# A decode step of attention and a gated MLP on one core: the last 192 rows of w_down loaded as 104 and 88 whole rows

## The chip, the cores and the metric

The kernel runs on one core of one Trainium2 chip. The metric is the device time of one execution in microseconds, as the median of several runs. All profile lines come from one profiled execution of the same program; times in them count from the start of its span.

## The reference, cut to what matters

```python
x = A_x                                                   # 1 x 640, bf16
h = x + A(layernorm(x), k_cache, v_cache, wq, wo)         # 32 heads, 4096 cached keys, head size 128
g, u = layernorm(h) @ w_gate, layernorm(h) @ w_up         # 640 -> 1728
h2 = h + (gelu(g) * u) @ w_down                           # 1728 -> 640
```

One token is computed. The two caches are 32 MB each, wq and wo 5 MB each, and the three MLP weights 2.2 MB each, so that 84 MB are read once and there is little arithmetic on each byte.

## The kernel before, in words

The order of the work is written out by hand: `Prog` (`P`) keeps one list of operations for each engine, `P.dma` adds a load, `V`, `A`, `T` and `GP` add work of VectorE, ScalarE, TensorE and GpSimd, and `emit` writes the lists out with one semaphore for each load. An operation waits for the events it is given. Within a list nothing overtakes.

All big loads are issued by SyncE, at line 59, in this order: wq into `arena`; sixteen K and V blocks of 4 MB into three `slots` in turn, the last V block in two halves; wo in three parts; and the MLP weights into the slots that have come free (`free[0]`, `free[1]`). A K block is multiplied by q on VectorE (L295), summed by TensorE against an identity (L28, L305), reduced (L313) and put through exp (L317); a V block is multiplied on TensorE (L336) and picked apart on VectorE (L353 to L363). Then come the projection by wo (L404), the sum with x, a layernorm (L258 to L264, L498) and the MLP.

The MLP's loads are issued in this order: two w_down loads for the rows from 1536 on (`d_wd[0]`, `d_wd[1]`), w_gate (`d_wg`), w_up in two parts (`d_wu`), and the first 1536 rows of w_down in four parts (`d_wd[2]` to `d_wd[5]`), the last of which is 128 rows of 1280 bytes. `wd_sb` holds w_down as 14 columns of 128 partitions by 640 numbers; columns 0 to 11 are the first 1536 rows.

`glu` (L509) makes g and u as rows, `turn` (L515 to L522) copies a row to SBUF and turns it by small matmuls into columns, 14 columns of 128 partitions. Lines 537 to 546 make gelu(g) times u, in `hm`, of 128 by 14. `down` (L553) multiplies column m of `hm` with column m of `wd_sb` and adds up in PSUM, as four pieces of 160 numbers. Two copies on VectorE (L566) and two on ScalarE (L568) bring the result to SBUF, and one store writes it.

In the kernel before, column 12 holds rows 1536 to 1663. The last 64 rows, of 1280 bytes each, are loaded as 128 half rows of 640 bytes, so that partition 2f has the first and partition 2f+1 the second half of row f. For that the 64 values of column 13 of `hm` are spread by one matmul with `sel2` over 128 partitions (`hp`, L557) and masked by `par` into the two columns of `hm2` (`h2`, L559), one for even partitions and one for odd ones. `sel2`, `par_t` and `par` are made at the start (L235, L238, L247). `z0` and `z1` (L496, L497) clear the part of column 13 that no matmul of `turn` writes.

Of the kernel before, what the change touches and what calls it, by code (L numbers as in the profile page):

```python
# [5 lines left out]
FP32 = mybir.dt.float32  # L6
BF16 = mybir.dt.bfloat16
ALU = mybir.AluOpType
ACTF = mybir.ActivationFunctionType
AX = mybir.AxisListType  # L10
# [8 lines left out]
GELU_C0 = math.sqrt(2.0 / math.pi)  # L19
GELU_C1 = 0.044715  # L20
NG = 8
NSLOT = 3


# [85 lines left out]
def bass_sequential_preLN__gqa_block_cached__glu_gated_geglu__decode_kernel(nc, A_x, A_k_cache, A_v_cache, A_wq, A_wo, B_x, B_w_gate, B_w_up, B_w_down, out):  # L110
    sb = lambda name, shape, dt: nc.alloc_sbuf_tensor(name, shape, dt)
    SLOT = 10 * DF
    slots = [sb("slot%d" % i, [128, SLOT], BF16) for i in range(NSLOT)]
    arena = sb("arena", [128, 5 * 4096], BF16)
    prod = sb("prod", [128, 4, 32, DH], BF16)
    qb = sb("qb", [128, NG, DH], BF16)
    sc = sb("sc", [128, 4, 32], FP32)
# [22 lines left out]
    rows = [sb("rows%d" % i, [128, 512], BF16) for i in range(2)]  # L140
    sel4 = sb("sel4", [128, 4], BF16)
# [4 lines left out]
    e_t = sb("e_t", [128, 14], FP32)  # L146
    gu = sb("gu", [128, 14], FP32)
    hm = sb("hm", [128, 14], BF16)
    hm2 = sb("hm2", [128, 2], BF16)
    sel2 = sb("sel2", [64, 64, 2], BF16)  # L150
    par_t = sb("par_t", [128, 2, 64], BF16)
    par = sb("par", [128, 2], FP32)
    one_bf = sb("one_bf", [1, 1], BF16)
    ones_f = sb("ones_f", [128, 128], FP32)
    mean_f = sb("mean_f", [128, 128], FP32)
    ones_b = sb("ones_b", [128, 1024], BF16)
# [9 lines left out]
    ps_g, ps_u = bank[0], bank[1]  # L166
    ps_q = [bank[4], bank[7]]
    ps_a = bank[4]
    ps_d = bank[4][:, 256:416]
    ps_s = bank[5]  # L170
    ps_z = bank[6]
    ps_p = bank[7]

    wo_sb = arena[:, :].rearrange("p (t i n) -> p t i n", t=2, i=16)
    view = lambda n: slots[n % NSLOT][:, 0:128 * DH].rearrange("p (g d) -> p g d", d=DH)

    P = Prog(nc)
    V = lambda fn, *d: P.op("vector", fn, *d)
    A = lambda fn, *d: P.op("scalar", fn, *d)
    T = lambda fn, *d: P.op("tensor", fn, *d)  # L180
    GP = lambda fn, *d: P.op("gpsimd", fn, *d)
# [4 lines left out]
    d_wq = [P.dma("sync", arena[:, :], A_wq[:, :].rearrange("(p c) n -> p (c n)", c=5))]  # L186
    order = [(kind, G) for G in range(NG - 2) for kind in "KV"] + [(kind, G) for kind in "KV" for G in (NG - 2, NG - 1)]
    pos = {t: n for n, t in enumerate(order)}
# [8 lines left out]
    def issue(upto):  # L197
        while state["next"] < min(upto, len(order)):
            n = state["next"]
            kind, g = order[n]  # L200
            src = A_k_cache if kind == "K" else A_v_cache
            src = src[0, 4 * g:4 * g + 4, :, :].rearrange("h (p r) d -> (h p) (r d)", p=32)
            dst = slots[n % NSLOT][:, 0:128 * DH]
            parts = 2 if n == len(order) - 1 else 1
            w = 128 * DH // parts
            landed[n] = [P.dma("sync", dst[:, i * w:(i + 1) * w], src[:, i * w:(i + 1) * w], consumed[n - NSLOT] if n >= NSLOT else None)
                         for i in range(parts)]
            state["next"] = n + 1

    issue(NSLOT)  # L210

# [6 lines left out]
    c_onesb = GP(lambda e: e.memset(ones_b[:, :], 1.0))  # L218
    c_idb = GP(lambda e: e.affine_select(id_b[:, :], ones_b[:, 0:128], pattern=[[1, 128]], compare_op=ALU.is_equal,
                                         fill=0.0, base=0, channel_multiplier=-1), c_onesb)  # L220
    c_idf = GP(lambda e: e.affine_select(id_f[:, :], ones_f[:, :], pattern=[[1, 128]], compare_op=ALU.is_equal,
                                         fill=0.0, base=0, channel_multiplier=-1), c_ones)
    c_sel = GP(lambda e: e.affine_select(sel[:, :, :], ones_b[0:16, :].rearrange("p (a b) -> p a b", a=8),
                                         pattern=[[-1, 8], [1, 128]], compare_op=ALU.is_equal,
                                         fill=0.0, base=0, channel_multiplier=-8), c_onesb)
    c_hz = GP(lambda e: e.memset(hs[:, :], 0.0))
    c_hs = GP(lambda e: e.affine_select(hs_t[:, :, :], ones_f[:, :].rearrange("p (a b) -> p a b", a=4),
                                        pattern=[[-1, 4], [-4, 32]], compare_op=ALU.is_equal,
                                        fill=0.0, base=0, channel_multiplier=1), c_ones)
    c_s4 = GP(lambda e: e.affine_select(sel4[:, :], ones_b[:, 0:4], pattern=[[-32, 4]], compare_op=ALU.is_equal,  # L230
                                        fill=0.0, base=0, channel_multiplier=1), c_onesb)
    c_m8 = GP(lambda e: e.affine_select(m8_t[:, :, :, :], ones_f[:, :].rearrange("p (a b c) -> p a b c", a=8, b=4),
                                        pattern=[[-4, 8], [-32, 4], [-1, 4]], compare_op=ALU.is_equal,
                                        fill=0.0, base=0, channel_multiplier=1), c_ones)
    c_sel2 = GP(lambda e: e.affine_select(sel2[:, :, :], ones_b[0:64, 0:128].rearrange("p (a b) -> p a b", a=64),  # L235
                                          pattern=[[1, 64], [0, 2]], compare_op=ALU.is_equal,
                                          fill=0.0, base=0, channel_multiplier=-1), c_onesb)
    c_par = GP(lambda e: e.affine_select(par_t[:, :, :], ones_b[:, 0:128].rearrange("p (a b) -> p a b", a=2),  # L238
                                         pattern=[[-1, 2], [-2, 64]], compare_op=ALU.is_equal,
                                         fill=0.0, base=0, channel_multiplier=1), c_onesb)  # L240
    c_pbd = GP(lambda e: e.memset(p_bd[:, :, :, :], 0.0))

    c_hs = V(lambda e: e.reduce_sum(hs[:, 12:16], hs_t[:, :, :], axis=AX.X), c_hs, c_hz)
    c_o4 = V(lambda e: e.reduce_max(ones4[:, :], sel4[:, :], axis=AX.X), c_s4)
    c_m8 = V(lambda e: e.reduce_sum(m8[:, :], m8_t[:, :, :, :].rearrange("p a b c -> p a (b c)"), axis=AX.X), c_m8)

    V(lambda e: e.reduce_sum(par[:, :], par_t[:, :, :], axis=AX.X), c_par)  # L247


    def x_cols(e):  # L250
# [20 lines left out]

    wq_j = arena[:, :].rearrange("p (c g j d) -> p c j g d", c=5, g=NG, j=4)

# [74 lines left out]
    def p_sum(G):  # L348
        sums[G] = V(lambda e: e.reduce_sum(RT[:, 4 * G:4 * G + 4], p_bd[:, G % 2, :, :].rearrange("p g j -> p j g"), axis=AX.X),  # L349
                    exps[4 * G + 3])  # L350
# [6 lines left out]
    def pick_sum(G):  # L357
        if G >= NG - 2:
            a1 = V(lambda e: e.tensor_add(po_m[:, 0:4, :], po_m[:, 0:4, :], po_m[:, 4:8, :]), mks[G])
# [56 lines left out]
    def scores(G):  # L416
# [7 lines left out]
        if G > 0:  # L424
            p_sum(G - 1)
        issue(pos[("K", G)] + 1 + NSLOT)

    headed = 0
    for kind, G in order:
# [14 lines left out]
        if G == 5:  # L444
# [10 lines left out]
    free = [consumed[len(order) - NSLOT + i] for i in range(1, 3)]  # L455
    wg_sb = sl[0][:, 0:5 * DF].rearrange("p (c n) -> p c n", c=5)
    wu_sb = sl[0][:, 5 * DF:10 * DF].rearrange("p (c n) -> p c n", c=5)
    wd_sb = sl[1][:, 0:14 * D].rearrange("p (m n) -> p m n", m=14)
    wu_v = B_w_up[:, :].rearrange("(p c) n -> p c n", c=5)
    wd_v = B_w_down[0:1536, :].rearrange("(a p r) n -> p a r n", a=3, r=4)  # L460
    wd_d = wd_sb[:, 0:12, :].rearrange("p (a r) n -> p a r n", a=3)
    d_wd = [P.dma("sync", wd_sb[:, 12, :], B_w_down[1536:1664, :], free[1]),
            P.dma("sync", wd_sb[:, 13, 0:320], B_w_down[1664:1728, :].rearrange("f (s n) -> (f s) n", s=2))]
    d_wg = P.dma("sync", wg_sb, B_w_gate[:, :].rearrange("(p c) n -> p c n", c=5), free[0])
    d_wu = [P.dma("sync", wu_sb[:, 0:3, :], wu_v[:, 0:3, :]),
            P.dma("sync", wu_sb[:, 3:5, :], wu_v[:, 3:5, :])]
# [2 lines left out]

    p_sum(NG - 1)  # L470
    pick(NG - 1)
    pick_sum(NG - 1)
# [10 lines left out]
    lo = [V(lambda e, t=t: e.tensor_sub(A_lo[0:97, 320 * t:320 * t + 320], bank[t][0:97, 0:320], A_hi[0:97, 320 * t:320 * t + 320]),  # L483
            hi[t]) for t in range(2)]
# [8 lines left out]
    T(columns(A_hi, True), *hi, c_o4)  # L493
    pr = T(columns(A_lo, False), *lo)
    h = V(lambda e: e.tensor_add(hT[:, 0:5], xx[:, 0:5], ps_p[:, 0:5]), pr)
    z0 = V(lambda e: e.memset(ps_g[64:128, 13:14], 0.0), lo[0])  # L496
    z1 = V(lambda e: e.memset(ps_u[64:128, 13:14], 0.0), lo[1])  # L497
    hl = layernorm(hT, h, lambda e: e.tensor_scalar(  # L498
        hlnT[:, :], hT[:, 0:5], ln[:, 0:1], ln[:, 4:5], ALU.subtract, ALU.mult))
    hx = V(lambda e: e.tensor_tensor(out=hX[:, :, :], in0=id_f[:, :].unsqueeze(2).to_broadcast([128, 128, 5]),  # L500
# [13 lines left out]
    def turn(k, ps, ev, z):  # L514
        cp = (V, A)[k](lambda e: (e.copy if k else e.tensor_copy)(rows[k][0:97, :], po[0:97, 512 * k:512 * k + 512]), ev)  # L515

        def fn(e):
            for r in range(4):
                i = e.matmul(ps[:, r:12:4], rows[k][0:97, r::4], sel4[0:97, 0:3], start=(r == 0), stop=True, skip_group_check=True)
            for m in (12, 13):  # L520
                n = 128 if m < 13 else 64
                i = e.matmul(ps[0:n, m:m + 1], rows[k][0:97, 128 * (m - 12):128 * (m - 12) + n], sel4[0:97, 3:4],  # L522
                             start=False, stop=True, skip_group_check=True)
            return i
        return T(fn, cp, z, c_s4)
# [20 lines left out]
    g9 = V(lambda e: e.tensor_mul(hm[:, :], gu[:, :], ps_u[:, 0:14]), g6, up)  # L546

    def down(ms, qs=range(4)):
        def fn(e):
            for m in ms:  # L550
                for q in qs:
                    h, n = (hm[:, m:m + 1], 160 * q) if m < 13 else (hm2[:, q // 2:q // 2 + 1], 160 * (q % 2))
                    i = e.matmul(ps_d[32 * q:32 * q + 1, 0:160], h, wd_sb[:, m, n:n + 160],  # L553
                                 start=False, stop=(m == 11))
            return i
        return fn
    hp = T(lambda e: e.matmul(ps_z[:, 0:1], sel2[:, :, :].rearrange("p a b -> p (a b)"), hm[0:64, 13:14],  # L557
                              start=True, stop=True), g9, c_sel2)
    h2 = V(lambda e: e.tensor_mul(hm2[:, :], par[:, :], ps_z[:, 0:1].to_broadcast([128, 2])), hp)  # L559
    T(down([12]), d_wd[0])  # L560
    T(down(range(4)), d_wd[2])
    T(down([13]), h2, d_wd[1])
    T(down(range(4, 8)), d_wd[3])
    T(down(range(8, 11)), d_wd[4])
    dn = {q: T(down([11], [q]), d_wd[5]) for q in (0, 2, 1, 3)}
# [36 lines left out]
```

## Time and profile before

| | us |
|---|---|
| median of 3 runs | 203.08 (203.05 to 203.18) |
| the profiled execution, its own time | 202.97 |
| its span, first to last instruction | 201.7 |
| TensorE busy in the span | 115.3 |
| VectorE busy | 129.5 |
| ScalarE busy | 51.3 |
| share of 16 DMA engines' time taken by the loads of SyncE | 97.9% |
| data read | 84.23 MB, 418 GB/s over the span |

The span is what the profile's lines cover; the execution's own time has 1.27 us more around it. The DMA engines are busy nearly all of the span, and every other engine has gaps. The loads of SyncE are shown as SPq lines at the time of their issue; a wait for data is shown as a wait on DMA with the name of the tile and the tensor.

### The profile page before, as it was taken

Reading aid. Unit: us, or ns where it says so; the run is one execution under the profiler, and the core shown is the slowest. Engines: PE = TensorE matmul, PEld = TensorE weight load, DVE = VectorE, ACT = ScalarE, POOL = GpSimd, SP = SyncE. Lnnn points to the kernel's source line nnn. Section 1 sums busy time; section 2 is a strip of 40 time slices with the busy share of each in tenths; the row PEclk is TensorE's granted clock in tenths of the full one; section 3 lists DMA queues with packets and bytes.
Section 4 is the critical chain, followed back from the end, with each engine's and each line's share of the span. In section 5 each row is a group of like instructions: output and inputs, shape, how many; then the busy total and the mean of one; then the engine's idle time right before and its main releaser. Section 6 shows DMA issues by size and latency. Waiting matters only on the chain.

```text
span 201.7 us, 1568 instructions
## 1 busy us (share of the span) xinstructions
PE 115.3 (57%) x788; PEld 17.0 (8%) x384; DVE 129.5 (64%) x136; ACT 51.3 (25%) x139; POOL 5.6 (3%) x15
## 2 busy tenths in 40 slices
PE   0108059536737775197529655876396097754564
PEld 0101000000001000000000001001000000121222
DVE  1300188517994898379857966896879979683341
ACT  2100003610560055005502440252025214500111
POOL 7300000000000000000000000000000000000000
PEclk9999756996996699859997978798569859997575
DMA  9999999999999999999999999999999999999992
GB/s 333 439 398 455 442 422 416 416 442 468 432 422 416 416 422 455 443 442 417 416 416 445 442 448 422 422 416 429 442 442 448 387 429 423 427 409 439 415 408 99
DMA packets 4330, 84.32 MB, mean 418 GB/s; under 512 B 482, under 2 KB 868, under 8 KB 1508
## 3 DMA queue, kind: packets, MB, share of 16 engines
q1 hardware_dynamic: 4322, 84.23, 97.9%
q8 instruction: 4, 0.07, 0.1%
q14 instruction: 2, 0.02, 0.0%
q10 hardware_dynamic: 2, 0.00, 0.0%
HBM read 84.23 MB, written 0.00 MB: 418 GB/s over the span
## 4 chain that ended last, share of the span: by engine, by line
DMA 52%; DVE 21%; PE 19%; issue 3%; ACT 2%; SPq 2%
DMA slot<-in_A_k_cache_dram 43%; DVE prod L295 16%; PE bank L28 13%; DMA slot<-in_B_w_down_dram 9%; DVE sc L313 3%; PE bank L336 3%; PE bank L305 2%; ACT p_bd L317 2%; SPq L59 2%; DVE po_r L363 1%; DVE po_m L353 1%; PE bank L553 0%; DVE out_row L566 0%; DVE RT L349 0%; DVE aP L393 0%
## 5 line engine op out<-in xcount | busy, mean ns | idle before, releaser
L295 DVE TENSOR_TENSOR prod<-slot,qb 128x4096 bf16<-128x4096 bf16 x32 | 72.4, 2283 | 24.3 <-DMA slot<-in_A_k_cache_dram 24.3
L317 ACT ACTIVATE p_bd<-sc,zero_t 32x32 bf16<-32x32 f32 x128 | 46.4, 362 | 107.7 <-DVE sc L313 106.5
L28 PE MATMUL bank<-prod,id_b 128*128 128x512 bf16 x224 | 68.6, 458 | 0.0
L305 PE MATMUL bank<-prod,id_b 128*128 128x512 bf16 x32 | 15.3, 477 | 45.2 <-DVE prod L295 45.1
L313 DVE TENSOR_REDUCE sc<-bank 128x32 f32<-128x512 f32 x32 | 22.0, 687 | 14.7 <-PE bank L28 14.7
L336 PE MATMUL bank<-slot,p_bd 128*32 128x512 bf16 x128 | 14.8, 448 | 15.0 <-ACT p_bd L317 13.8
L28 PE MATMUL bank<-slot,p_bd 128*32 128x512 bf16 x128 | 14.9, 453 | 0.0
L305 PEld LDWEIGHTS bank<-prod,id_b 128*128 128x128 bf16 x32 | 3.5, 109 | 108.6 <-DVE prod L295 108.6
L363 DVE TENSOR_REDUCE po_r<-po_m 128x128 f32<-128x1024 f32 x6 | 11.2, 1867 | 0.0
L353 DVE TENSOR_TENSOR po_m<-bank,m 128x1024 f32<-128x1024 f32 x8 | 9.7, 1214 | 0.6 <-PE bank L28 0.6
L280 PE MATMUL bank<-arena,xlnB 128*32 128x512 bf16 x20 | 3.3, 628 | 7.2 <-DMA arena<-in_A_wq_dram 7.2
L285 DVE CAST qb<-bank 128x512 bf16<-128x512 f32 x1 | 0.7, 692 | 10.0 <-PE bank L28 10.0
L336 PEld LDWEIGHTS bank<-slot,p_bd 128*32 128x32 bf16 x128 | 3.8, 106 | 35.7 <-ACT p_bd L317 26.1
L509 PE MATMUL bank<-slot,hlnT 128*1 128x512 bf16 (+1 forms) x40 | 4.0, 486 | 2.7 <-DVE hX L500 2.2
L349 DVE TENSOR_REDUCE RT<-p_bd 128x4 f32<-128x512 bf16 x8 | 5.4, 675 | 0.0
L252 PE MATMUL bank<-one_bf,x_row 1*128 1x1 bf16 x5 | 0.4, 177 | 7.1 <-DMA x_row<-in_A_x_dram 7.1
L369 PE MATMUL bank<-po_r,hs 128*16 128x128 f32 x16 | 3.4, 301 | 1.5 <-DVE po_r L361 1.5
L286 ACT CAST qb<-bank 128x512 bf16<-128x512 f32 x1 | 0.6, 586 | 10.4 <-PE bank L28 10.4
L28 PE MATMUL bank<-arena,xlnB 128*32 128x512 bf16 x20 | 3.2, 613 | 0.0
L404 PE MATMUL bank<-arena,aP 128*1 128x320 bf16 x32 | 2.5, 314 | 1.1 <-DMA arena<-in_A_wo_dram 1.1
L263 ACT ACTIVATE ln<-ln,eps_t 128x1 f32<-128x1 f32 x2 | 0.6, 294 | 9.4 <-DVE ln L261 9.4
L482 ACT CAST A_hi<-bank 97x320 bf16<-97x320 f32 x1 | 0.4, 426 | 9.8 <-PE bank L28 9.8
(87 smaller groups left out, 42.9 us busy)
## 6 DMA issues: line engine op xcount, KB each, us to landing
slot<-in_A_k_cache_dram SPq DMA_DIRECT2D x8, 4096.0 KB, 21.0
slot<-in_A_v_cache_dram SPq DMA_DIRECT2D x7, 4096.0 KB, 17.7
arena<-in_A_wq_dram SPq DMA_DIRECT2D x1, 5120.0 KB, 15.5
slot<-in_A_v_cache_dram SPq DMA_DIRECT2D x2, 2048.0 KB, 14.9
arena<-in_A_wo_dram SPq DMA_DIRECT2D x1, 2560.0 KB, 22.9
slot<-in_B_w_gate_dram SPq DMA_DIRECT2D x1, 2160.0 KB, 11.0
arena<-in_A_wo_dram SPq DMA_DIRECT2D x1, 1920.0 KB, 27.0
slot<-in_B_w_up_dram SPq DMA_DIRECT2D x1, 1296.0 KB, 13.7
```

What stands on the lines that cost most here:

```text
L28: return e.add_instruction(mybir.InstMatmult(name=nc.get_next_instruction_name(), engine=e.engine, start_tensor_calc=start, stop_tensor_ca ...
L59: ev = self.op(eng, lambda e: e.dma_start(out, in_), *deps, dma=True)
L295: m = V(lambda e: e.tensor_tensor(out=prod[:, s % 4, :, :], in0=kt[:, 32 * u:32 * u + 32, :], in1=qb[:, G, :].unsqueeze(1).to_broadcast([1 ...
L305: i = e.matmul(*args, start=True, stop=False)
L313: reds[s] = V(lambda e: e.reduce_sum(sc[:, s % 4, :], ps_f[s % 2][:, :].rearrange("p (g d) -> p g d", d=16), axis=AX.X), folds[s], exps.ge ...
L317: x = A(lambda e, j=j: e.activation(p_bd[32 * j:32 * j + 32, G % 2, 32 * (s % 4):32 * (s % 4) + 32, j], sc[32 * j:32 * j + 32, s % 4, :], ...
L336: return e.matmul(*args, start=(c < 4), stop=(c >= 12))
L349: sums[G] = V(lambda e: e.reduce_sum(RT[:, 4 * G:4 * G + 4], p_bd[:, G % 2, :, :].rearrange("p g j -> p j g"), axis=AX.X), exps[4 * G + 3])
L353: mks[G] = V(lambda e: e.tensor_tensor(out=po_m[:, :, :], in0=po[:, :].rearrange("p (b d) -> p b d", b=8), in1=m8[:, :].unsqueeze(2).to_br ...
L363: evs[G] = V(lambda e: e.reduce_sum(po_r[:, G % 2, :], po_m[:, :, :].rearrange("p b d -> p d b"), axis=AX.X), mks[G], hds.get(G - 2))
L369: return e.matmul(ps_a[0:16, 128 * (G // 4):128 * (G // 4) + 128], hs[:, 12 - 4 * g:28 - 4 * g], po_r[:, G % 2, :], start=(g == 0), stop=( ...
L509: i = e.matmul(po[32 * a:32 * a + 1, 512 * k:512 * k + n], hlnT[:, c:c + 1], w[:, c, 512 * a:512 * a + n], start=(c == 0), stop=(c == 4))
```

## The change

The 192 rows from 1536 on are loaded as 104 whole rows onto partitions 0 to 103 of column 12 and 88 whole rows onto partitions 0 to 87 of column 13. `turn` makes column 12 with 104 and column 13 with 88 values, `z0` and `z1` clear the upper 64 partitions of both columns ahead of it, and `down` sums over 104 and 88 partitions for these two. `hp`, `h2`, `hm2`, `sel2`, `par_t` and `par` go away. On TensorE `down([12, 13])` now stands first and waits for both loads.

```diff
+TAIL = ((1536, 104), (1640, 88))
...
-    c_sel2 = GP(lambda e: e.affine_select(sel2[:, :, :], ones_b[0:64, 0:128].rearrange("p (a b) -> p a b", a=64),
...
-    c_par = GP(lambda e: e.affine_select(par_t[:, :, :], ones_b[:, 0:128].rearrange("p (a b) -> p a b", a=2),
...
-    V(lambda e: e.reduce_sum(par[:, :], par_t[:, :, :], axis=AX.X), c_par)
...
-    d_wd = [P.dma("sync", wd_sb[:, 12, :], B_w_down[1536:1664, :], free[1]),
-            P.dma("sync", wd_sb[:, 13, 0:320], B_w_down[1664:1728, :].rearrange("f (s n) -> (f s) n", s=2))]
+    d_wd = [P.dma("sync", wd_sb[0:n, 12 + i, :], B_w_down[lo:lo + n, :], free[1]) for i, (lo, n) in enumerate(TAIL)]
...
-    z0 = V(lambda e: e.memset(ps_g[64:128, 13:14], 0.0), lo[0])
-    z1 = V(lambda e: e.memset(ps_u[64:128, 13:14], 0.0), lo[1])
+    z0 = V(lambda e: e.memset(ps_g[64:128, 12:14], 0.0), lo[0])
+    z1 = V(lambda e: e.memset(ps_u[64:128, 12:14], 0.0), lo[1])
...
-            for m in (12, 13):
-                n = 128 if m < 13 else 64
-                i = e.matmul(ps[0:n, m:m + 1], rows[k][0:97, 128 * (m - 12):128 * (m - 12) + n], sel4[0:97, 3:4],
+            for m, (lo, n) in zip((12, 13), TAIL):
+                i = e.matmul(ps[0:n, m:m + 1], rows[k][0:97, lo - 1536:lo - 1536 + n], sel4[0:97, 3:4],
...
+                k = 128 if m < 12 else TAIL[m - 12][1]
                 for q in qs:
-                    h, n = (hm[:, m:m + 1], 160 * q) if m < 13 else (hm2[:, q // 2:q // 2 + 1], 160 * (q % 2))
-                    i = e.matmul(ps_d[32 * q:32 * q + 1, 0:160], h, wd_sb[:, m, n:n + 160],
+                    i = e.matmul(ps_d[32 * q:32 * q + 1, 0:160], hm[0:k, m:m + 1], wd_sb[0:k, m, 160 * q:160 * q + 160],
...
-    hp = T(lambda e: e.matmul(ps_z[:, 0:1], sel2[:, :, :].rearrange("p a b -> p (a b)"), hm[0:64, 13:14],
-                              start=True, stop=True), g9, c_sel2)
-    h2 = V(lambda e: e.tensor_mul(hm2[:, :], par[:, :], ps_z[:, 0:1].to_broadcast([128, 2])), hp)
-    T(down([12]), d_wd[0])
+    T(down([12, 13]), g9, *d_wd[0:2])
     T(down(range(4)), d_wd[2])
-    T(down([13]), h2, d_wd[1])
```

More of the change, by code (lines that the diff above doesn't have):

```diff
@@ L148, in bass_sequential_preLN__gqa_block_cached__glu_gated_geglu__decode_kernel @@
     hm = sb("hm", [128, 14], BF16)
[L149 to L152, printed above, removed]
     one_bf = sb("one_bf", [1, 1], BF16)
@@ L234, in bass_sequential_preLN__gqa_block_cached__glu_gated_geglu__decode_kernel @@
                                         fill=0.0, base=0, channel_multiplier=1), c_ones)
-    c_sel2 = GP(lambda e: e.affine_select(sel2[:, :, :], ones_b[0:64, 0:128].rearrange("p (a b) -> p a b", a=64),
-                                          pattern=[[1, 64], [0, 2]], compare_op=ALU.is_equal,
-                                          fill=0.0, base=0, channel_multiplier=-1), c_onesb)
-    c_par = GP(lambda e: e.affine_select(par_t[:, :, :], ones_b[:, 0:128].rearrange("p (a b) -> p a b", a=2),
-                                         pattern=[[-1, 2], [-2, 64]], compare_op=ALU.is_equal,
-                                         fill=0.0, base=0, channel_multiplier=1), c_onesb)
     c_pbd = GP(lambda e: e.memset(p_bd[:, :, :, :], 0.0))
```

## The prediction

> **What bounds the kernel now.** I read the page's slices and queues first.
>
> ```profile
> DMA  9999999999999999999999999999999999999992
> GB/s 333 439 398 455 442 422 416 416 442 468 432 422 416 416 422 455 443 442 417 416 416 445 442 448 422 422 416 429 442 442 448 387 429 423 427 409 439 415 408 99
> DMA packets 4330, 84.32 MB, mean 418 GB/s; under 512 B 482, under 2 KB 868, under 8 KB 1508
> q1 hardware_dynamic: 4322, 84.23, 97.9%
> q10 hardware_dynamic: 2, 0.00, 0.0%
> ```
>
> The DMA engines are at nine tenths or more in 39 of 40 slices: the load stream never pauses, so its last load sets the end and work on other engines is cover. Next, from the end of the chain of waits (start, us, step):
>
> ```profile
> 180.84 18.22 DMA slot<-in_B_w_down_dram
> ```
>
> It ends at 199.06. Then the end of the timeline (start, us, instruction, and in brackets the idle time before it):
>
> ```profile
> 179.90 1.85 SPq L59 DMA_DIRECT2D slot<-in_B_w_down_dram  x4
> 196.83 0.17 PE L557 MATMUL bank<-hm,sel 64*128 64x1 bf16 x1 [0.33 <-DVE hm L546]
> 196.94 0.71 PE L553 MATMUL bank<-slot,hm 128*1 128x160 bf16 x24
> 197.04 0.16 DVE L559 TENSOR_TENSOR hm<-par,bank 128x2 bf16<-128x2 f32 x1 [0.27 <-PE bank L557]
> 197.95 0.70 PE L553 MATMUL bank<-slot,hm 128*1 128x160 bf16 x16 [0.30 <-DMA slot<-in_B_w_down_dram]
> 199.10 0.70 PE L553 MATMUL bank<-slot,hm 128*1 128x160 bf16 x16 [0.45 <-DMA slot<-in_B_w_down_dram]
> 199.49 0.09 PEld L553 LDWEIGHTS bank<-slot,hm 128*1 128x1 bf16 x4 [0.16 <-DMA slot<-in_B_w_down_dram]
> ```
>
> TensorE waits three times at its end for w_down, 0.30, 0.45 and 0.16 us; only four matmuls, the copies and the store follow the last landing.
>
> A load is done when every engine with a share of it is done. The trace keeps the sixteen increments of each load's semaphore. Of the last load (128 rows of 1280 B), in us of the span:
>
> ```
> 197.74 197.82 197.89 197.93 198.00 198.08 198.10 198.18
> 198.23 198.44 198.90 199.03 199.25 199.28 199.30 199.44
> ```
>
> Sixteen engines run each at its own pace, the last 1.70 us behind the first. The packets say why: an engine moves 40960 B in 1514 ns with no gap (27.05 GB/s; sixteen make 433), and four instruction loads of 16 KB, at 53.9, 109.7, 174.8 and 193.5 us, each put one engine some 1.5 us behind. It never catches up. So the end is the end of one late engine, and what counts is what that engine has to do.
>
> **The change, part by part.**
>
> The loads: bytes stay at 245,760. Before, each engine has eight packets of 1280 B and eight of 640 B. Their packets last 55 and 32 ns and overlap by a few ns; between the increments of consecutive loads an engine spends 0.44 us on the eight of 1280 B and 0.20 us on the eight of 640 B, 0.64 in all. How 104 and 88 rows are shared out no row shows. The two near ones: a 128-row load has sixteen semaphore packets, and the one-row load of x two packets in all (q10), one of data, one semaphore. So a load goes over as many engines as its rows fill with equal shares; the most for 104 is 13, with eight rows each, and for 88 is 11, with eight. [...]
>
> Counting both from the same first engine, engines 0 to 10 have sixteen packets of 1280 B, 0.88 us in place of 0.64: +0.24. Engines 11 and 12 have eight: -0.20. Engines 13 to 15 have none: -0.64. The last engine's place among them is not in the trace. [...] So each late one has 10 chances in 15 to be among 1 to 10. If the last is (two in three), +0.24. If it is spared, the next three, 199.25 to 199.30, are all spared in only one case in a hundred, so the end is 199.30 + 0.24 = 199.54, +0.10. The ends of this term are what six engines from 198.90 on allow when five of them sit in 11 to 15: 198.90 + 0.24 for the sixth, -0.30 at best; and +0.24. I take +0.24.
>
> Where the rows land: in every load before, each engine has its own eight partitions, always the same for a 128-row load. Shares of 13 and 11 are cut elsewhere, on 104 and 88 partitions, so a late engine writes 16 rows into partitions that other engines, most of them over 1.2 us ahead, are at that moment filling with w_gate at their full rate. Whether 27.05 GB/s is the limit of the engine or of the place written to, the trace cannot tell. If the engine's, nothing is added. If the place's, each of the two gets half, and the late engine's sixteen packets take 0.88 us more. The slowed neighbours have the time to spare. No row lies between; the nearest is the rate of all sixteen engines, equal to under 1% over 40960 B packets although each reads its own rows, which looks like a fixed limit on the path to SBUF. I lean to the upper end: three quarters, +0.66, ends 0 and 0.88. [...]
>
> Fewer engines than 13 and 11 would make this dearer: eight for both, as 13 and 11 rows each, is 24 packets or 1.32 us, +0.68 before any sharing; one engine, as for x, 192 packets of 55 ns, +9.9. The spread's floor is zero: 192 rows evenly are 12 packets, 0.66 for 0.64.
>
> SyncE: two issues at 177.62 take 0.81 us; the odd shape may cost what x's issue cost on ScalarE, 0.49 for 0.33, +0.16 each. The first engine reaches these loads at 181.46, and the w_gate issue behind them ends at 178.90, so 2.5 us cover it. The six loads behind shift with it, all issued by 181.7 and the last started at 196.8. Nothing on the path; without cover +0.32.
>
> TensorE and VectorE at the end: `hp` (0.17 us), its weight load (0.09) and `h2` (0.16) go. `down` ran on beside them from 196.94 and then waited 0.30 us for w_down, so they hid behind that load: 0; without it -0.3. `down([12, 13])` waits for both tail loads, which landed at 184.19 and 184.37, twelve us before `hm`: 0, and if it were late all of `down` would queue behind it. The turning matmuls (L522, 163 to 213 ns) change from 128 and 64 columns to 104 and 88, the memsets from 64x1 to 64x2 (0.06 us each), below 0.05 us either way, and the waits for w_down absorb it.
>
> The start: two selects on GpSimd (0.71 and 0.30 us, from 4.84) and a sum on VectorE (0.29, at 5.84) go. x lands at 7.08 and wq is waited for until 15.66, so 0; no more than 1.0 if that cover were gone.
>
> Sum: 0.24 + 0.66 = +0.90 on the last landing, with TensorE, the copies and the store behind it unchanged: 202.97 + 0.90 = 203.87 for a profiled execution. The median of the runs stands 0.11 above it: 203.98, say 204.0.
>
> **Rivals.** A measurement here tells 0.2%, 0.41 us, from no change.
>
> Uneven shares alone (0.28): the place costs nothing, the last engine pays 0.10 to 0.24: 203.2 to 203.3, within 0.2%. For it: each load of the trace keeps the same rate whatever its packet size. Against: no load of before has two engines at the same partitions.
>
> The late engines are spared (0.08): the change takes 0.64 us off three engines and 0.20 off two, and if the six late ones sit there, or a slightly shorter program moves an instruction load off the last one, the end comes sooner. Best by the shares alone -0.30, 202.8, from five of the six late engines in the top five places on. With the instruction load of 174.8 us on an engine with time to spare, five are late, 198.90 to 199.30: all in the top five places, they end by 199.03 - 0.20 = 198.83, -0.61, 202.5, past the bound. I price all of it as faster.
>
> Fewer engines (0.06): the shares are not 13 and 11 but at most 8, so the change does not keep the loads spread: +0.68 with free places, up to 205.3 with all 24 packets shared (+0.68 + 1.32 = +2.00, on 203.08 is 205.08), and +9.9 for one engine, 213.0.
>
> The forecast keeps 0.58: +0.5 to +1.12.
>
> **How the numbers follow.** 204.0 is the likeliest case. Slower is the forecast and the fewer engines, 0.64; same 0.28; faster 0.08. The forecast's own range is 203.6 to 204.2; the range 203.1 to 205.0 takes in the uneven shares above their middle and eight engines, and leaves out the gain, the lowest of the uneven shares and the one-engine end, together under 0.2.
>
> **What would show it.** Packets under 512 B: 482 less 5 for 104 and 3 for 88 rows is 474; under 2 KB, 796; in all 4258. Sixteen equal shares would leave 482. The increments of the first tail load would be thirteen, of the second eleven. Right: packets of 1280 B in the tail well over 55 ns on some engines, the chain's last DMA step ending near 199.96, TensorE still waiting for it. Uneven shares alone: packets stay at 55 ns and the last landing is 199.5 to 199.7. Wrong altogether: the last landing before 199.3, the wait of TensorE for w_down gone, or a pause in the DMA slices.

## The result, and the profile after

| | before | after |
|---|---|---|
| median of the runs, us | 203.11 (203.05 to 203.57, 6 runs) | 204.33 (204.16 to 204.47, 6 runs) |
| the profiled execution, us | 202.97 | 204.32 |
| its span, us | 201.7 | 203.1 |
| last increment of the last load, us of the span | 199.45 | 200.80 |

The changed kernel is slower: 1.0057 times the time of before (95% interval 1.0044 to 1.0070), +1.22 us in the medians and +1.35 in the two profiled executions. The load stream still ends the kernel. From the page of after, slices and packets:

```profile
DMA  9999999999999999999999999999999899999991
GB/s 363 403 421 458 413 413 433 445 458 420 410 413 452 458 426 413 421 439 434 452 413 423 420 439 452 433 413 433 426 439 458 381 426 448 406 387 376 406 410 76
DMA packets 4258, 84.32 MB, mean 415 GB/s; under 512 B 474, under 2 KB 796, under 8 KB 1436
q1 hardware_dynamic: 4250, 84.23, 97.8%
```

The bytes are the same, and the packets are 474, 796 and 4258, as 13 and 11 semaphore packets for the two loads ask. The 36th and 37th slice moved 387 and 376 GB/s, for 409 and 439 before. The same stretch of both kernels in the view by windows; the columns are the window, its length, busy time and count of each engine, TensorE's granted clock, the DMA engines' busy share and GB/s. The view counts a packet whole where it starts, so a share can pass 1. Before:

```profile
core 0: us, PE busy (x) PEld busy (x) DVE busy (x) ACT busy (x) POOL busy (x), PEclk, DMA share, GB/s
182.00:187.00 5.00, 2.60 (x43) 1.17 (x28) 1.73 (x7) 0.43 (x1) 0.00 (x0) 0.66 1.08 449
```

After:

```profile
182.00:187.00 5.00, 2.81 (x37) 0.77 (x22) 1.38 (x3) 0.42 (x1) 0.00 (x0) 0.56 1.07 358
```

The DMA engines are as busy, 1.07 for 1.08, and move a fifth less, 358 GB/s for 449. (With only the part of each packet that lies in the window it is 331 for 421, the same loss.) Those 91 GB/s over 5 us are 455 KB, or 1.1 us at the 418 GB/s of the whole span before: by this estimate most of the loss lies here. The end of the chain of waits of after, then from the timelines one line of before and the end of after:

```profile
180.78 19.62 DMA slot<-in_B_w_down_dram
```

```profile
183.77 0.43 PE L404 MATMUL bank<-arena,aP 128*1 128x320 bf16 x4 [0.53 <-DMA arena<-in_A_wo_dram]
```

```profile
184.79 0.43 PE L393 MATMUL bank<-arena,aP 128*1 128x320 bf16 x4 [0.41 <-DMA arena<-in_A_wo_dram]
...
198.65 1.50 PE L540 MATMUL bank<-slot,hm 104*1 104x160 bf16 x40 [0.33 <-DVE hm L533]
200.44 0.71 PE L540 MATMUL bank<-slot,hm 128*1 128x160 bf16 x16 [0.28 <-DMA slot<-in_B_w_down_dram]
200.85 0.09 PEld L540 LDWEIGHTS bank<-slot,hm 128*1 128x1 bf16 x4 [0.18 <-DMA slot<-in_B_w_down_dram]
```

The chain's DMA step ends at 200.40, 1.34 us later than before. The line of before and the first one of after are the projection's last part: it waits for the wo load that stands ahead of the changed ones in the queue and starts at 184.79, where before it started at 183.77. So a load of which nothing was changed already lands 1.02 us late.

The packets of the tail in the two traces (ns; the tail is the packets of the two loads for the left-over rows; w_gate is the load behind them, the third part of wo the one ahead):

```
                        before                after
tail, 1280 B            128, mean 55,  max 58   192, mean 82,  max 131
w_gate, 17280 B         128, mean 650, max 681  128, mean 733, max 1115
third part of wo, 5120  128, mean 199, max 205  128, mean 222, max 396
```

All three kinds are slower; the slowest packet lasts 1.6 to 2.3 times as long as the slowest of before.

The packets also tell what single engines did. In both traces a packet starts within some 10 ns of the end of the one before it on the same engine, so for the engines that come last the packets can be put in line. In us of the span:

```
              before, last engine   after, last engine   after, last on wo
wo, part 3    181.68 to 183.25      181.42 to 183.77     181.88 to 184.18
tail          183.25 to 183.91      183.76 to 184.91     no packet
w_gate        183.91 to 189.07      184.90 to 190.38     184.18 to 189.63
```

After the change the engine that comes last on wo has no packet of the tail: from 183.90 on the packets of the tail come one after the other, so from one engine, and several of them start while the last on wo is still writing wo; its own next packet, at 184.18, is one of w_gate. Last from there on is an engine that was 0.46 us ahead of it at the start of this part of wo and has sixteen packets of the tail. Against the last engine of before it started 0.26 us earlier, spent 0.77 us more on wo, 0.49 more on the tail and 0.32 more on w_gate, and is 1.31 us behind at the end of w_gate, where the last landing is 1.35 later.

Part 1 of wo, which lands ahead of the first packet of the changed loads, has its last increment at 177.72, where before it was 177.51. Over the profiled executions of all the kernels here that time lies between 177.47 and 177.80, in no order with the loss, so 0.2 us at this point is no more than one trace differs from another.

### The profile page after: what moved, and what is told of

Its sections match the earlier page's. It is cut to its first block, busy times and chain, and to the rows that moved or that the text cites. A ratio compares the mean times of both kernels' runs of the same rounds, so it can differ in the third digit from the quotient of the medians.

```text
span 203.1 us, 1561 instructions
## 1 busy us (share of the span) xinstructions
PE 115.4 (57%) x787; PEld 17.4 (9%) x383; DVE 129.0 (64%) x134; ACT 51.3 (25%) x139; POOL 4.7 (2%) x13
## 2 busy tenths in 40 slices
DMA packets 4258, 84.32 MB, mean 415 GB/s; under 512 B 474, under 2 KB 796, under 8 KB 1436
## 4 chain that ended last, share of the span: by engine, by line
DMA 52%; DVE 20%; PE 19%; issue 4%; ACT 2%; SPq 2%
DMA slot<-in_A_k_cache_dram 43%; DVE prod L284 15%; PE bank L29 13%; DMA slot<-in_B_w_down_dram 10%; DVE sc L302 3%; PE bank L325 3%; PE bank L294 2%; ACT p_bd L306 2%; SPq L60 2%; DVE po_r L352 1%; DVE po_m L342 1%; PE bank L540 0%; DVE out_row L549 0%; DVE RT L338 0%; DVE aP L382 0%
## 5 line engine op out<-in xcount | busy, mean ns | idle before, releaser
L29 PE MATMUL bank<-prod,id_b 128*128 128x512 bf16 x224 | 66.2, 445 | 0.0
L294 PE MATMUL bank<-prod,id_b 128*128 128x512 bf16 x32 | 15.0, 468 | 47.1 <-DVE prod L284 47.1
L325 PE MATMUL bank<-slot,p_bd 128*32 128x512 bf16 x128 | 15.8, 482 | 15.0 <-ACT p_bd L306 13.8
L29 PE MATMUL bank<-slot,p_bd 128*32 128x512 bf16 x128 | 15.6, 476 | 0.0
L269 PE MATMUL bank<-arena,xlnB 128*32 128x512 bf16 x20 | 3.0, 577 | 7.1 <-DMA arena<-in_A_wq_dram 7.1
L497 PE MATMUL bank<-slot,hlnT 128*1 128x512 bf16 (+1 forms) x40 | 4.8, 552 | 2.8 <-DMA slot<-in_B_w_gate_dram 2.6
L393 PE MATMUL bank<-arena,aP 128*1 128x320 bf16 x32 | 3.0, 373 | 1.3 <-DMA arena<-in_A_wo_dram 1.3
L29 PE MATMUL bank<-arena,aP 128*1 128x320 bf16 x32 | 3.1, 385 | 0.0
L29 PE MATMUL bank<-arena,xlnB 128*32 128x512 bf16 x20 | 3.0, 574 | 0.0
```

What stands on the lines that cost most here:

```text
L29: return e.add_instruction(mybir.InstMatmult(name=nc.get_next_instruction_name(), engine=e.engine, start_tensor_calc=start, stop_tensor_ca ...
L294: i = e.matmul(*args, start=True, stop=False)
L325: return e.matmul(*args, start=(c < 4), stop=(c >= 12))
L497: i = e.matmul(po[32 * a:32 * a + 1, 512 * k:512 * k + n], hlnT[:, c:c + 1], w[:, c, 512 * a:512 * a + n], start=(c == 0), stop=(c == 4))
```

## The experiments

Two theories stood against the forecast's sharing of places: the uneven shares of 13 and 11 engines, and the work of TensorE and VectorE (`hp`, `h2` and the new order of `down`). A place is here, as the prediction takes it, the group of partitions that one engine writes in a load of 128 rows; no trace names it. All times below are medians with the ratio to runs of the kernel before on the same chip (203.10, 203.13 and 203.00 us in the three groups of runs). The packet times are those of the tail's 1280 B packets in the profiled execution.

**Even shares, cut elsewhere.**

```diff
-TAIL = ((1536, 104), (1640, 88))
+TAIL = ((1536, 112), (1648, 80))
```

> The change with loads of 112 and 80 rows in place of 104 and 88: equal shares of 7 and 5 rows on all sixteen engines (482 packets under 512 B), 12 packets of 1280 B each, but cut at other partitions than a 128-row load. Shared places (two engines writing into the same group of partitions slow each other): packets of 1280 B in the tail well over 55 ns, w_gate packets over 644 ns on some engines, time +0.7 to +1.2 us on the kernel before, 203.8 to 204.3. Uneven shares alone: no engine has more than the others, packets at 55 ns, 203.1 (+0.02). Removed hp and h2 or the order of down as the cause: as the changed kernel, 204.3, with packets at 55 ns.

204.34 us, 1.0057 (1.0042 to 1.0072): the loss of the change, with 482 small packets, so sixteen equal shares. That is just above the range expected for shared places. Packets mean 78, at most 124 ns, and those of w_gate mean 742, at most 1205. The same window:

```profile
182.00:187.00 5.00, 2.81 (x37) 0.76 (x21) 1.33 (x4) 0.43 (x1) 0.00 (x0) 0.56 1.07 347
```

347 GB/s at the busy share of before. The uneven shares are not needed for the loss.

**Sixteen packets on every engine, in the places of before.**

```diff
-TAIL = ((1536, 104), (1640, 88))
+TAIL = ((1536, 128), (1600, 128))
...
-                k = 128 if m < 12 else TAIL[m - 12][1]
+                p = 64 if m == 13 else 0
...
-                    i = e.matmul(ps_d[32 * q:32 * q + 1, 0:160], hm[0:k, m:m + 1], wd_sb[0:k, m, 160 * q:160 * q + 160],
+                    i = e.matmul(ps_d[32 * q:32 * q + 1, 0:160], hm[p:128, m:m + 1], wd_sb[p:128, m, 160 * q:160 * q + 160],
```

> The change with two loads of 128 whole rows, from row 1536 and from row 1600; of the second only partitions 64 to 127 are used, so that 64 rows are read twice. Every engine has sixteen packets of 1280 B, as the fullest have in the changed kernel, and each writes its own partitions; hp and h2 are gone as in the change. Shared places: packets at 55 ns, +0.24 us on the kernel before, 203.35. Uneven shares alone, with all that the change cost on the path put down to sixteen packets on the late engine: 204.3, as the changed kernel. Removed hp and h2 or the order of down as the cause: 204.3 too, with packets at 55 ns.

203.39 us, 1.0016 (1.0006 to 1.0025): +0.29, for 64 rows more to read. Packets mean 57, at most 69 ns. The tail takes the last engine 0.85 us by its increments (183.97 on wo, 184.82 on the tail), where before it took 0.64: +0.21 for sixteen packets in place of eight and eight half ones.

```profile
182.00:187.00 5.00, 3.01 (x43) 1.04 (x26) 1.82 (x8) 0.43 (x1) 0.00 (x0) 0.54 1.06 438
```

With loads of 128 partitions the rate is back at 438 GB/s, though the other engines run the changed kernel's code without `hp` and `h2`. So that code is not the cause.

**The tail behind all other loads,** with the changed loads and with those of before. The edit of the first of the two, in its main lines; the mark that ends a sum (`stop`) moves to column 13 with it.

```diff
-    d_wd = [P.dma("sync", wd_sb[0:n, 12 + i, :], B_w_down[lo:lo + n, :], free[1]) for i, (lo, n) in enumerate(TAIL)]
...
-    d_wd += [P.dma("sync", wd_d[:, a, lo:hi, :], wd_v[:, a, lo:hi, :])
+    d_wd = [P.dma("sync", wd_d[:, a, lo:hi, :], wd_v[:, a, lo:hi, :], free[1])
...
+    d_wd = [P.dma("sync", wd_sb[0:n, 12 + i, :], B_w_down[lo:lo + n, :], free[1]) for i, (lo, n) in enumerate(TAIL)] + d_wd
...
-    T(down([12, 13]), g9, *d_wd[0:2])
-    T(down(range(4)), d_wd[2])
+    T(down(range(4)), g9, d_wd[2])
...
-    dn = {q: T(down([11], [q]), d_wd[5]) for q in (0, 2, 1, 3)}
+    T(down([11]), d_wd[5])
+    dn = {q: T(down([12, 13], [q]), *d_wd[0:2]) for q in (0, 2, 1, 3)}
```

> The changed kernel with its loads of 104 and 88 rows behind all others, and their matmuls last. The late engine then writes its sixteen rows when most other engines are done, so hardly anyone shares with it. Against the next kernel, which has the loads of the kernel before at the same place: shared places +0.0 to +0.4 us (sixteen packets against eight and eight half ones, little sharing left for the last engine); a cost of the loads that does not hang on who else is writing: +1.2 us as in the change.

> The kernel before with its loads of 128 rows and 128 half rows behind all others, and their matmuls last: the control for the kernel above. Same bytes on each engine, so within 0.3 us of the kernel before by every theory, 203.0 to 203.4; eight matmuls in place of four behind the last landing are some 0.1 us of it.

204.13 us, 1.0048 (1.0031 to 1.0064), against 203.27 us, 1.0008 (0.9999 to 1.0017) for the control. The control did as expected. The changed loads cost 0.86 us at this place, where 0.0 to 0.4 was expected, a miss: the expectation took hardly anyone to be still at work beside the late engine. By the increments of the load ahead, seven engines still finish that load between 198.2 and 199.6 us. The trace shows both sides: up to the one that starts at 199.23 us, packets of 74 to 122 ns stand among those of 55, and the last eight, from 199.38 on, one after the other and so from one engine, last 55 ns each. Eight rows are a whole share, cut as in the change. So a share is not slow by its cut. It is slow while others are writing too.

**64 rows, on partitions 32 to 95 and on partitions 0 to 63.**

```diff
-TAIL = ((1536, 104), (1640, 88))
+TAIL = ((1536, 128), (1664, 64))
+LOADS = ((1536, 128, 0), (1664, 64, 32))
...
-    d_wd = [P.dma("sync", wd_sb[0:n, 12 + i, :], B_w_down[lo:lo + n, :], free[1]) for i, (lo, n) in enumerate(TAIL)]
+    d_wd = [P.dma("sync", wd_sb[at:at + n, 12 + i, :], B_w_down[lo:lo + n, :], free[1]) for i, (lo, n, at) in enumerate(LOADS)]
```

The three numbers of `LOADS` are first row, rows and first partition. In this first kernel `turn` writes column 13 by two matmuls to partitions 32 to 63 and 64 to 95, the rest of that column is cleared, and `down` sums 96 partitions of it. The second kernel has the line of `TAIL` alone.

> 128 whole rows as in the kernel before, and the last 64 rows whole, on partitions 32 to 95; hp and h2 gone. 12 packets of 1280 B on each of sixteen engines. [...] If any load that is not 128 partitions is slowed by its cut alone: packets well over 55 ns, +0.4 us or more. [...]

> The same with the 64 rows on partitions 0 to 63. Same packets, same shares of four rows, another place. [...]

On 32 to 95: 203.12 us, 0.9997 (0.9988 to 1.0006), packets mean 56, at most 62 ns. On 0 to 63: 203.72 us, 1.0028 (1.0017 to 1.0039), packets mean 62, at most 132 ns. The windows, in this order:

```profile
182.00:187.00 5.00, 2.60 (x44) 1.43 (x28) 1.88 (x8) 0.42 (x1) 0.00 (x0) 0.72 1.06 444
```

```profile
182.00:187.00 5.00, 2.44 (x42) 0.95 (x26) 1.53 (x4) 0.42 (x1) 0.00 (x0) 0.62 1.05 393
```

Same bytes read from the same rows, same packets, and each of the sixteen engines has four of the 64 rows; 32 partitions of shift are worth 0.6 us. So the cost is on the side that is written. The trace does not name the partitions of a packet, so which engines were in each other's way is not shown.

**96 and 96 rows, with the second load from partition 32 or from 0 on.**

```diff
-TAIL = ((1536, 104), (1640, 88))
+TAIL = ((1536, 96), (1600, 128))
+LOADS = ((1536, 96, 0), (1632, 96, 32))
```

This first kernel loads by `LOADS` as above, and `down` sums partitions 32 to 127 of column 13. The second has both loads from partition 0 on:

```diff
-TAIL = ((1536, 104), (1640, 88))
+TAIL = ((1536, 96), (1632, 96))
```

> 96 whole rows on partitions 0 to 95 and 96 on partitions 32 to 127, six rows each engine and load. [...] If it counts that two engines write into one place at once, whatever its total: +0.6 to +1.2 us, as with 112 and 80 rows.

> [...] If only sharing at a time counts: both alike.

204.16 us, 1.0046 (1.0029 to 1.0062), and 204.08 us, 1.0042 (1.0027 to 1.0057): alike within their intervals, and at +1.03 and +0.95 us both in the range expected if it counts that two engines write into one place at once. Packets mean 77 and 78, at most 116 and 169 ns. How many rows come to a place in each of the two is not shown, so they do not decide whether the total at a place counts. That two engines write into one place at the same time fits the runs here; as no trace names a packet's partitions, it is concluded from them and not seen.

**The changed shares, from partition 32 on.**

```diff
-LOADS = ((1536, 128, 0), (1664, 64, 32))
+LOADS = ((1536, 52, 32), (1588, 52, 32), (1640, 44, 32), (1684, 44, 32))
```

This is an edit of the kernel with 64 rows on partitions 32 to 95. `wd_sb` gets two more columns for the four loads, `down([12, 13])` waits for all four, and its sums leave out columns 14 and 15. In shares of four rows the loads take 13, 13, 11 and 11 engines, so that one engine has at most sixteen packets.

> [...] Uneven shares cost little: packets at 55 ns, +0.1 to +0.24 us on the kernel before, 203.2 to 203.4, the last landing set by whichever late engine has sixteen packets. Uneven shares as the main cost of the change: +0.8 to +1.2 us, 203.9 to 204.3. Two more issues on SyncE cost nothing by either.

203.23 us, 1.0010 (1.0001 to 1.0020): +0.23. Packets mean 56, at most 66 ns, and the page counts 498 packets under 512 B, which are 482 less the 32 of the two tail loads of before and 13, 13, 11 and 11 for these four.

```profile
182.00:187.00 5.00, 2.62 (x52) 1.32 (x32) 1.91 (x8) 0.43 (x1) 0.00 (x0) 0.76 1.04 437
```

With uneven shares like those of the change, but packets of 56 ns, the kernel loses 0.23 us and keeps a rate of 437 GB/s. So the uneven shares are not the main cost.

It was expected that an engine with sixteen packets would end last; the trace does not bear that out. The engine that comes last on wo has no packet of the tail here either. The next one takes 0.86 us for its sixteen, and w_gate lands at 189.52, where it landed at 189.51 before. The last landing falls behind only at the second part of w_up, 2.50 us after the first part where before it was 2.11; in that time, from 192.93 us on, stands an instruction load of 16 KB. So another engine, most likely the one that this load held up, ends the kernel.

## Why the prediction was right, and where its sizes were off

The forecast was slower by 0.90, 204.0 us; it came out at +1.22. That is above the +0.5 to +1.12 of the forecast's own range and inside the wider one. Step by step:

- **What bounds the kernel.** The load stream, by its late engines: shown. The span ends 2.25 to 2.28 us behind the last landing in all the kernels here, but for the two that have the tail last, with 2.47 and 2.49, so what moved the time moved the last landing.
- **The shares.** 13 and 11 engines: shown, by the counts of small packets and by the 14 and 12 increments the trace has for the two loads, one for each engine and one more, at 178.23 and 178.62, right behind the issue and over 4 us ahead of the others.
- **Uneven shares, +0.24.** The price of sixteen packets was nearly right: 0.85 and 0.86 us in the two kernels whose tail packets stayed at 57 and 56 ns, for 0.64, so +0.21. That both loads count from the same engine, and where the late engines stand in that count, no run shows: there +0.24 and its two in three were the author's assumption. But in the profiled execution of the changed kernel the engine that came last on wo has no packet of the tail, which is part of the case to which the prediction gave one in three, and the one that ends last started 0.26 us earlier than that of before. So the shares by themselves are worth about 0.21 - 0.26 = -0.05 us there, an estimate from these times. Whether other executions spare the same engine is not shown.
- **Shared places, +0.66 of at most 0.88.** That packets slow when the shares are cut elsewhere is shown, a mean of 82 ns for 55; the term was mis-sized: with 112 and 80 rows, where every engine has the same share, the kernel loses 1.24, above the upper end. The bound counted the late engine's own sixteen packets and said that the slowed neighbours have the time to spare. That step failed. The late engine is itself a slowed neighbour, on the loads ahead and behind: of its time, 0.77 us more than before went to wo, 0.32 to w_gate, and only 0.28 to its own tail beyond the longer share, in all 1.37 in place of 0.66. The packets of wo begin to slow at 181.6 us, right after the first ones of the tail at 181.32. That they slow because the engines ahead write into the late engine's place fits the runs, but no trace names the places, and that two engines at one place get half the rate each, from which the 0.88 was taken, no run shows.
- **The sum.** Part of its nearness is luck: it put the sharing 0.7 us too low and, as far as this one trace shows, the shares 0.3 too high.
- **TensorE and VectorE at the end, SyncE, the start: 0.** With 64 rows on partitions 32 to 95 `hp`, `h2`, `sel2` and `par` are gone and the time is that of before, 0.9997, so they hid behind the loads. The two changed issues on SyncE took 0.73 us together, less than the 0.81 of before, and with two further ones, in the kernel of four loads, the kernel loses no more than 0.23.
- **The rivals.** Uneven shares alone would have been 203.2 to 203.3, and the kernel with 13, 13, 11 and 11 engines from partition 32 on measures 203.23; as its trace gives another reason for that, the agreement shows no more than that this cause is small. An engine that was late was spared, as the second rival had it, but the next one, whose packets were slower, ended last in its stead. Fewer engines is ruled out by the increments.
- **Slips.** The 5 and 3 packets less belong the other way round, 3 to the 104 rows and 5 to the 88; the sum of 474 is right. The 205.3 of the rival with fewer engines should be the 205.08 that is worked out beside it.

Not settled is what the place is in the hardware, and which partitions each engine has in loads of 104 and 88 rows; no trace here shows a packet's partitions. The split of the loss between wo, tail and w_gate is that of one execution, with the packets put in line by their times.

## What to carry to other kernels

In a kernel that is bound by its loads, do not count a load's cost by bytes and engines alone: look at which partitions it writes while the other loads run at full rate. Here loads of 104 and 88 rows in the middle of the stream slowed their neighbours as well, wo ahead of them (a mean of 222 ns for 199) and w_gate behind them (733 for 650). With 112 and 80 rows w_gate took 742, and with 96 and 96 the window from 182 to 187 us moved 359 and 360 GB/s for 449. Using all sixteen engines evenly did not help: 204.34 us with 112 and 80 rows. Not every load of fewer than 128 partitions slows them: 64 left-over rows on partitions 32 to 95 were as fast as the half rows (203.12 us) and needed no matmul to spread the values.

The last increments of two loads need not be those of one engine: after the change the one that ended last on wo, at 184.18, had no packet of the tail. Before a loss is split up by them, put the packets of the late engines in line.

## What the runs showed of the hardware

- A busy DMA engine is not a moving one: in the window from 182 to 187 us the busy share was 1.08 before and 1.07 after, at 449 and 358 GB/s by the same count. A packet that is slowed counts as busy for all of its time.
- A share of eight rows is not slow by its shape: with the tail behind all other loads, its last eight packets took 55 ns each once the other engines were done, while packets a little earlier took up to 122 ns.
- Moving a 64-row load by 32 partitions changed the time by 0.6 us, 203.12 for 203.72, with every packet count on the page the same (482 under 512 B, 4266 in all).
